# A 300-try search over instruction priorities, with new cost constants and a new load order, in a scheduled RWKV-7 and MLP kernel

## The chip, the cores and the metric

The kernel runs on one core of a Trainium2 chip. The metric is the device time of one launch in microseconds, lower is better. A core has five instruction queues that run side by side: PE (matrix multiply), DVE (vector), ACT (scalar functions), POOL (general purpose) and SP, which here does nothing but issue DMAs. Each queue executes its own instructions strictly in the order in which they stand, and waits on semaphores for the others.

## The reference

Two stages: a recurrent attention layer over 4 batches, 8 heads and 768 steps with head size 40, then an MLP with a quick GELU over the 3072 tokens that come out of it, 320 to 2048 to 320. Activations of the first stage arrive as float32, the MLP's weights as float64.

```python
for t in range(S):
    y[:, :, t] = einsum('bhd,bhde->bhe', rt, state)
    Sa = einsum('bhde,bhe->bhd', state, at)
    state = state * wt[:, :, None, :] - einsum('bhd,bhe->bhde', Sa, bt) + einsum('bhd,bhe->bhde', vt, kt)
x = y.transpose(0, 2, 1, 3).reshape(B * S, H * D)
h = x @ w_in
return (h / (1 + exp(-1.702 * h))) @ w_out
```

## The kernel before

**Tiling.** The 768 steps are cut into 12 chunks of 64, and the 4 batches into 2 pairs. A chunk of one pair is a *unit*, so there are 24 units. Unit i needs the state left by unit i-2. For each unit `decay` takes logarithms and exponentials of w, `prep` scales a, b, k and forms the score matrices (`ps_A`, `ps_RV`), `inverse` inverts a triangular matrix in five dependent levels (`ps_level`), and `solve` brings in the state (`ps_zT`, `ps_rz`, `ps_B`), solves (`ps_X`) and produces the output and the next state (`ps_y`). The output goes through a DRAM scratch (`x_dram`) and comes back transposed as `xT_all`. After both units of a chunk, `mlp` does 4 blocks of up-projection (`ps_up`, then the GELU into `g` on ACT), and two output tiles of down-projection (`ps_down`).

**Weights.** The eight pieces of float64 weights, 1.31 MB each, are loaded raw and rebuilt as float32 by one ACT instruction (L422) and five of DVE (L426, L430, L431, L434, L438). Piece n may land in a buffer that an earlier piece used (`raws`, `spots`).

**The plan.** The order of the work is not written by hand. Each piece of work is a `Task` with a priority (its *rank*, lower first), estimated durations for the engines that may do it, and dependences. `Plan.order` simulates the engines at build time: at each moment it gives each free engine the able task of lowest rank, decides the engine for tasks that may go to several, and books PSUM pairs. Its model has constants for the time in which the PE's instructions are fetched (256 at a time, `BLOCK`, `FETCH`; slower beside DMAs, `BESIDE`), for when each engine begins, and for DMA latency and rate. `Plan.paced` (L205) calls `order` four times, moving release times of the MLP tasks, and keeps the plan whose simulated end is earliest. The list it returns is emitted task by task, so that it alone fixes the order of each of the five queues. SP's queue too: a load stands in line behind all loads planned before it, and behind their waits for free buffers.

**The start.** Before the planned tasks come hand-ordered ones: the input buffers `ak`, `b`, `rv` (two of each) are set to zero once, since the loads fill only 40 of 64 rows. DVE clears the first of each and POOL the second, after it has built all masks:

```python
    for t in ak_t[1], b_t[1], rv_t[1]:
        padded(nc.gpsimd, t)
```

`load(i)` (L466 and after) plans the five loads of a unit in the order ak, time, b, rv, RV.

Of the kernel before, what the change touches and what calls it, by code (L numbers as in the profile page):

```python
# [23 lines left out]
ACT = mybir.ActivationFunctionType  # L24
# [34 lines left out]
class Plan:  # L59
# [2 lines left out]

    BLOCK, FETCH, BESIDE, AHEAD = 256, 3550.0, 0.4, 300.0
    DELAY = {"PE": 300.0, "DVE": 60.0, "ACT": 60.0, "POOL": 150.0, "SP": 800.0}

    BEGIN = {"PE": 0.0, "ACT": 3300.0, "DVE": 4100.0, "POOL": 9500.0, "SP": 800.0}
    LATENCY, RATE, SPREAD = 1200.0, 400.0, 1.3

    def __init__(self, slots, pairs):
        self.slots, self.pairs = slots, pairs
        self.tasks, self.made, self.used, self.of_pair = [], {}, {}, {}

    def add(self, rank, engines, fn, reads=(), uses=(), writes=(), room=(), pair=None, most=None, size=0):

        t = Task(rank, engines, fn, pair, most, size)
        for key in uses:  # L80
            self.used.setdefault(key, []).append(t)
        for key in reads:
            t.after.update(self.made[key])
            self.used.setdefault(key, []).append(t)
        for name, n in (*writes, *room):
            if name in self.slots:
                old = (name, n - self.slots[name])
                t.after.update(self.made.get(old, ()), self.used.get(old, ()))
        for key in writes:
            self.made.setdefault(key, []).append(t)  # L90
        if pair is not None:
            writers = self.of_pair.setdefault(pair, [])
            t.after.update(o for o in writers if "PE" in o.engines)
            writers.append(t)
        t.after.discard(t)
        self.tasks.append(t)

    def order(self):
        for n, t in enumerate(self.tasks):
            t.n, t.left, t.ready, t.then = n, len(t.after), 0.0, []  # L100
        for t in self.tasks:
            for o in t.after:
                o.then.append(t)
        free = dict(self.BEGIN)
        pairs = [0.0] * self.pairs
        held, users = {}, {k: len(v) for k, v in self.of_pair.items()}
        coming = [(t.release, t.n) for t in self.tasks if not t.left]
        heapq.heapify(coming)
        able, now, wire, out, many = [], 0.0, 0.0, [], set()
        running, last = [], {}  # L110

        def fits(t):
            if t.pair is None or t.pair in held:
                return True
            clear = sum(p <= now for p in pairs)
            if t.most is None:

                return clear > len({o.pair[0] for o in able if o.most is not None and o.pair not in held and not any(k[0] == o.pair[0] for k in many)})
            return clear > 0 and sum(k[0] == t.pair[0] for k in many) < t.most

        issued, begun, shared = 0, 0.0, 0.0

        def fetch(at):
            took = self.FETCH
            for _ in range(3):
                beside = sum(max(0.0, min(y, at + took) - max(x, at)) for x, y in running[-8:])
                took = self.FETCH + self.BESIDE / self.SPREAD * beside
            return took

        def unread(t, e):  # L130

            return max((x + 60.0 for o, x in last.get(t.pair, {}).items() if o != e), default=0.0) if t.pair is not None and e != "PE" else 0.0

        def fetched(t, start):

            at, left, ns, block = start, t.instr, t.engines["PE"] / t.instr, begun
            room = self.BLOCK - issued % self.BLOCK
            while left >= room:
                at += room * ns
                left -= room  # L140
                at = block = max(at, block + fetch(block))
                room = self.BLOCK
            return at + left * ns, block

        def ahead(t):

            return (issued % self.BLOCK + t.instr) * fetch(begun) / self.BLOCK - (now + t.engines["PE"] - begun)

        while coming or able:
            while coming and coming[0][0] <= now:  # L150
                able.append(self.tasks[heapq.heappop(coming)[1]])
            able.sort(key=lambda t: (t.rank, t.n))
            took = None
            for e in free:
                if free[e] <= now:
                    took = next((t for t in able if e in t.engines and fits(t) and unread(t, e) <= now), None)
                    if took and e == "PE" and ahead(took) > self.AHEAD:

                        took = next((t for t in able if e in t.engines and fits(t) and ahead(t) < min(self.AHEAD, ahead(took))), took)
                    if took:  # L160
                        break
            if not took:
                later = [x for x in (*free.values(), *pairs, *(unread(t, e) for t in able for e in t.engines)) if now < x < float("inf")]
                now = min(later + ([coming[0][0]] if coming else []))
                continue
            t = took
            able.remove(t)
            t.engine = e
            end = now + t.engines[e]
            if e == "PE":  # L170
                end, begun = fetched(t, now)
                issued += t.instr
            if e == "POOL" or e == "DVE" and t.sbuf:

                shared = max(now, shared) + t.engines[e]
                end = max(end, shared)
            free[e] = end
            if e == "SP":
                wire = max(wire, end + self.LATENCY)
                running.append((wire, wire + self.SPREAD * t.size / self.RATE))  # L180
                end = wire = running[-1][1]
            if t.pair is not None:
                if e != "PE":
                    last.setdefault(t.pair, {})[e] = end
                if t.pair not in held:
                    held[t.pair] = next(i for i, p in enumerate(pairs) if p <= now)
                    pairs[held[t.pair]] = float("inf")
                    if t.most is not None:
                        many.add(t.pair)
                t.bank = held[t.pair]  # L190
                users[t.pair] -= 1
                if not users[t.pair]:
                    many.discard(t.pair)
                    pairs[t.bank] = end + self.DELAY[e]
            for o in t.then:
                o.ready = max(o.ready, end + (0.0 if o.engines.keys() == {e} else self.DELAY[e]))
                o.left -= 1
                if not o.left:
                    heapq.heappush(coming, (max(o.ready, o.release), o.n))
            t.start = now  # L200
            out.append(t)
        assert len(out) == len(self.tasks)
        return out

    def paced(self, groups, rounds, window, share):  # L205
# [15 lines left out]
            vars(t).update(kept)  # L221
        return [t for t, _ in best[1]]


@with_exitstack
def rwkv7_gelu_quick(ctx: ExitStack, tc: tile.TileContext, time_d, v_d, w_d, wc_d, ak_d, b_d, rv_d, w_in, w_out, out):
    nc = tc.nc
    H, D, S = 8, 40, out.shape[0] // 4
    DM = H * D
# [11 lines left out]
    BY_PE = 4  # L241
    PLAIN = 4
    ROUNDS, WINDOW, SHARE = 4, 5000.0, 1.0
    RANKS = [14, 16, 20, 24, 35, 37, 39, 41]
    HALF = [slice(0, 64), slice(64, 128)]
    BITS = (0, 1)
# [58 lines left out]
    def padded(engine, t):  # L305
        engine.memset(t, 0.0)
# [10 lines left out]
    nc.vector.tensor_add(two32, one32, one32)  # L317
    padded(nc.vector, b_t[0])
    padded(nc.vector, rv_t[0])

    def select(t, compare, base, sign, fill):

# [13 lines left out]
    for t in logw_t:  # L336
        nc.gpsimd.memset(t[:, DM:], 0.0)

    starts = single("starts", [128, 8, 33])
    nc.gpsimd.memset(starts, 1.0)  # L340
    nc.gpsimd.memset(starts[:, :, 0], 0.0)

    quads, within = single("quads", [128, 2, 32]), single("within", [128, 2, 32])
    nc.gpsimd.memset(quads, 0.0)
# [9 lines left out]
        for p in HALF:  # L354
            select(t[p, :64], ALU.is_gt, 0, 1, 0.0)

    for t in ak_t[1], b_t[1], rv_t[1]:
        padded(nc.gpsimd, t)

    def mask(t):  # L360
        return t.unsqueeze(1).unsqueeze(1).to_broadcast([128, 2, 4, 64])
# [100 lines left out]
    def load_w(i):  # L462
        for name, of, src, n in (("wc", wc_of, wc_d, 528), ("logw", logw_of, w_d, DM))[i < BY_PE:]:
            plan.add(-2 if i == 2 else 10 * i - 30, {"SP": 350.0}, lambda t, of=of, src=src: nc.sync.dma_start(of(i), src[i]),
                     writes=[(name, i)], size=128 * n * 4)

    def load(i):
        for name, of, src, n in (("ak", ak_of, ak_d, 1024), ("time", time_of, time_d, 2 * DM), ("b", b_of, b_d, 512),
                                 ("rv", rv_of, rv_d, 1024), ("RV", RV_of, v_d, 320)):
            rows = [slice(p.start, p.start + D) for p in HALF] if name in ("ak", "b", "rv") else [slice(0, 128)]  # L470

            def go(t, name=name, of=of, src=src, rows=rows):
                for p in rows:
                    dst = of(i)[p, 8:].rearrange("p g j n -> p (g j n)") if name == "RV" else of(i)[p]
                    nc.sync.dma_start(dst, src[i, p])
            plan.add(10 * i - 4, {"SP": 350.0 * len(rows)}, go, writes=[(name, i)] + ([("v", i)] if name == "RV" else []),
                     size=sum(p.stop - p.start for p in rows) * n * 4)


    G_of = lambda i: buf("G", i, [128, 2, 160])  # L480
# [520 lines left out]
    for t in plan.tasks:  # L1001
        if t.rank >= 10000 and "PE" in t.engines:
            paces.setdefault(t.rank // 100, []).append(t)
    tasks = plan.paced(list(paces.values()), ROUNDS, WINDOW, SHARE)
    for t in tasks:
        t.fn(t)

# [80 lines left out]
```

## Time and profile before

| | us |
|---|---|
| median of 3 runs | 725.19 |
| the runs | 728.75, 724.26, 725.19 |
| the profiled execution, as timed | 728.5 |
| its span in the trace | 726.7 |

| engine | busy us | share of the span |
|---|---|---|
| PE matmul | 677.6 | 93% |
| PE weight load | 572.5 | 79% |
| DVE | 430.0 | 59% |
| ACT | 356.8 | 49% |
| POOL | 187.9 | 26% |

A row of the profile names the source line, the engine, the operation, what is written from what is read with partitions x elements, the count and the mean. Since nearly all matmuls go through one helper, they are told apart by the PSUM tile that they write. The float32 matmul of the source is two records in the trace, and each has a weight load with it. The instruction queues are themselves filled by DMA; the profile lists those packets as queue kind "instruction", and they are 16,384 bytes each.

| tile | records | columns |
|---|---|---|
| ps_up | 3840 | 256 |
| ps_down | 3072 | 320 |
| ps_level | 4000 | 32 to 128 |
| ps_y, ps_B, ps_X | 3776 | 104 |
| ps_N, ps_RV, ps_A, ps_T, ps_Q, ps_zT, ps_rz | 5248 | 32 to 64 |
| ps_cum, ps_cumc | 320 | 160, 65 |

### The profile page before, as it was taken

How to read it: one execution, taken by the hardware profiler on the slowest of the kernel's cores; microseconds unless marked ns; L12 is line 12 of the kernel's file. 1: busy time of each engine (PE TensorE's matmuls, PEld its weight loads, DVE VectorE, ACT ScalarE, POOL GpSimd, SP SyncE). 2: the span in 40 equal slices, each digit the busy share in tenths (PEclk: the TensorE clock that was granted, in tenths of full speed). 3: DMA queues.
4: the chain of work that ended last, by engine and by line, in shares of the span. 5: the costliest groups of instructions: out<-in, count | busy, mean ns of one | idle time of the engine just before them, and what ended most of it. 6: DMA issues, size and time to landing. Idle time of an engine off the chain costs nothing.

```text
span 726.7 us, 43527 instructions
## 1 busy us (share of the span) xinstructions
PE 677.6 (93%) x20256; PEld 572.5 (79%) x20256; DVE 430.0 (59%) x739; ACT 356.8 (49%) x705; POOL 187.9 (26%) x260
## 2 busy tenths in 40 slices
PE   4566997999999999999999999999999989999997
PEld 4555885799788789888888878887889978897564
DVE  6578888956667666666756655755666556431000
ACT  4455655557554554545465455457446446342120
POOL 8104143432431331330350320431530310200000
PEclk9879998999999999999999999999999999999999
DMA  7963542332251341351450440441340230110000
GB/s 216 351 251 93 165 124 86 107 96 78 91 145 55 109 120 49 88 158 32 119 136 22 116 130 31 119 118 39 120 112 23 85 95 5 40 49 30 18 5 20
DMA packets 31861, 69.82 MB, mean 96 GB/s; under 512 B 5056, under 2 KB 14272, under 8 KB 30656
## 3 DMA queue, kind: packets, MB, share of 16 engines
q1 hardware_dynamic: 31680, 67.03, 30.5%
q8 instruction: 159, 2.61, 1.4%
q14 instruction: 22, 0.18, 0.1%
HBM read 59.15 MB, written 7.86 MB: 92 GB/s over the span
## 4 chain that ended last, share of the span: by engine, by line
PE 83%; DVE 5%; issue 3%; ACT 3%; DMA 3%; POOL 2%; SPq 1%; POOLq 0%; DVEq 0%; ACTq 0%
PE ps_down L275 28%; PE ps_up L275 26%; PE ps_level L275 8%; PE ps_y L275 5%; PE ps_B L275 4%; PE ps_X L275 2%; DMA ak<-in_ak 2%; PE ps_Q L275 2%; PE ps_N L275 1%; PE ps_T L275 1%; PE ps_rz L275 1%; PE ps_A L275 1%; PE ps_RV L275 1%; PE ps_zT L275 1%; PE ps_cum L275 1%
## 5 line engine op out<-in xcount | busy, mean ns | idle before, releaser
L275 PE MATMUL ps_up<-xT_all,w_sb 64*64 64x256 f32 x3840 | 249.1, 378 | 2.6 <-ACT g L942 1.5
L275 PE MATMUL ps_down<-w_sb,g 64*64 64x320 f32 x3072 | 244.4, 434 | 3.1 <-DVE w_sb L438 2.5
L275 PEld LDWEIGHTS ps_up<-xT_all,w_sb 64*64 64x64 f32 x3840 | 160.6, 133 | 26.7 <-ACT g L942 1.8
L275 PEld LDWEIGHTS ps_down<-w_sb,g 64*64 64x64 f32 x3072 | 136.2, 134 | 45.3 <-issue 3.1
L670 ACT ACTIVATE EX<-ES,quads 128x256 f32<-128x256 f32 x116 | 52.6, 501 | 49.7 <-DVE ES L665 49.3
L591 POOL TENSOR_TENSOR kh<-time,G 128x320 f32<-128x320 f32 x24 | 22.0, 918 | 185.3 <-PE ps_y L275 91.4
L942 ACT ACTIVATE g<-ps_up 128x1024 f32<-128x1024 f32 x48 | 49.1, 1023 | 40.4 <-PE ps_up L275 40.1
L275 PEld LDWEIGHTS ps_level<-W,EX 64*64 64x64 f32 x2560 | 57.3, 134 | 7.4 <-ACT EX L670 1.4
L716 DVE TENSOR_TENSOR E<-two,ps_level 128x256 f32<-128x256 f32 x80 | 33.2, 415 | 40.3 <-ACT W L714 39.8
L275 PE MATMUL ps_level<-W,EX 64*64 64x64 f32 (+1 forms) x2560 | 55.7, 218 | 0.7 <-ACT EX L670 0.3
L714 ACT COPY W<-ps_level 128x512 f32<-128x512 f32 x51 | 29.8, 585 | 44.0 <-PE ps_level L275 43.9
L275 PE MATMUL ps_level<-PT,EX 64*64 64x64 f32 (+2 forms) x1280 | 36.6, 251 | 11.4 <-DVE EX L686 7.2
L968 DVE TENSOR_TENSOR ob<-ob,ps_down 128x320 f32<-128x320 f32 x24 | 11.6, 484 | 59.4 <-ACT ob L966 59.1
L275 PEld LDWEIGHTS ps_level<-PT,EX 64*64 64x64 f32 x1280 | 34.3, 152 | 15.2 <-DVE EX L686 7.0
L907 POOL TENSOR_TENSOR x<-zr,FT 128x128 f32<-128x128 f32 x84 | 42.8, 539 | 10.4 <-ACT zr L899 10.2
L583 POOL TENSOR_TENSOR ak<-ak,FT 128x512 f32<-128x512 f32 x21 | 27.3, 1299 | 53.2 <-DMA ak<-in_ak 26.2
L845 ACT COPY B<-ps_B 128x416 f32<-128x416 f32 x36 | 18.2, 506 | 44.1 <-PE ps_B L275 43.6
L275 PE MATMUL ps_y<-RV,kh 64*64 64x104 f32 x768 | 36.4, 252 | 2.3 <-DVE M L861 2.2
L665 DVE STREAM_TRANSPOSE ES<-E 128x256 f32<-128x256 f32 x80 | 35.6, 445 | 3.9
L275 PE MATMUL ps_y<-M,bh 64*64 64x104 f32 x768 | 36.5, 252 | 1.3 <-issue 1.3
L275 PEld LDWEIGHTS ps_y<-RV,kh 64*64 64x64 f32 x768 | 30.1, 134 | 6.4 <-DVE M L861 2.4
L861 DVE TENSOR_TENSOR M<-ps_X,later 128x832 f32<-128x832 f32 x24 | 24.5, 1021 | 17.6 <-PE ps_X L275 17.6
(140 smaller groups left out, 1132.9 us busy)
## 6 DMA issues: line engine op xcount, KB each, us to landing
ak<-in_ak SPq DMA_DIRECT2D x48, 160.0 KB
time<-in_time SPq DMA_DIRECT2D x24, 320.0 KB
rv<-in_rv SPq DMA_DIRECT2D x48, 160.0 KB
xT_all<-x_dram SPq DMA_DIRECT2D x48, 160.0 KB
wc<-in_wc SPq DMA_DIRECT2D x20, 264.0 KB
logw<-in_w SPq DMA_DIRECT2D x24, 160.0 KB
b<-in_b SPq DMA_DIRECT2D x48, 80.0 KB
RV<-in_v SPq DMA_DIRECT2D x24, 160.0 KB
```

The source lines that it names most:

```text
L275: nc.tensor.matmul(o, lhsT, rhs, start=start, stop=True, skip_group_check=True)
L583: plan.add(R, {"DVE": 690.0, "POOL": 1270.0, "sbuf": True}, lambda t: of(t.engine).tensor_mul(ahT(), ahT(), FT_of(i)), reads=T("ak", "FT") ...
L591: plan.add(R + 4, {"POOL": 870.0, "DVE": 490.0, "sbuf": True}, lambda t, n=n, dst=dst: of(t.engine).tensor_mul(dst(i)[:, :, :D], by_head(t ...
L665: plan.add(rank, dve(256), lambda t: nc.vector.transpose(ES(n), source(t)), writes=[key("ES", n, 6)], **reads)
L670: nc.scalar.activation(dst[:, :, h], ES(n), ACT.Copy, scale=quads[:, h, :1])
L714: plan.add(rank, any2(512), lambda t: copy(t.engine)(tiles_of(W(n + 1)), blocks(psum(t, ""), 64)), writes=[key("W", n + 1, 5)], pair=pair)
L716: plan.add(rank, dve(256), lambda t: nc.vector.tensor_sub(tiles_of(E(n + 1)), every(two32, [128, 2, 4, 32]), blocks(psum(t, ""), 64)[:, :, ...
L845: plan.add(R, any2(416), lambda t: copy(t.engine)(dst(), psum(t, "")[:, :, :208]), writes=[("Bv", i)] if x and c > 0 else T("B"), pair=(na ...
L861: plan.add(R + 1, dve(832), lambda t: nc.vector.tensor_tensor(M_of(i).rearrange("p (j b) n -> p b j n", b=2), psum(t, "")[:, :, :416].rear ...
L907: of(t.engine).tensor_mul(x[:, b ^ u, b], both(i)[:, at, :64], FT_of(i)[:, at])
L942: plan.add(-45, act(1024), lambda t: nc.scalar.activation(g_of(c * NQ + q).rearrange("p m r n -> p r m n"), psum(t, "").rearrange("p r (m ...
L968: plan.add(-45, dve(320), lambda t: nc.vector.tensor_add(ob_of(serial), ob_of(serial), psum(t, "")[:, 1, :DM]), reads=[("ob", serial)], wr ...
```

## The change

It does not change what is computed: the same 20,256 matmul records are issued in both programs. Five things move.

1. The constants of the model. The fetch, DMA and begin times are refitted; large loads (over 1 MB) slow the fetch more than small ones (`BESIDE_LARGE`); matmul work counts double when the PE was busy for less than 45% of the last 2.6 us (`takes`).
2. The start: DVE clears the second `b` and `rv` (`ak` stays on POOL but stands ahead of the masks), and the mask `starts` is built last.
3. The load order in a unit: ak, b, rv, RV, time; and each of the first six small loads gets a release time (`CLEAR`).
4. After `paced`, `refined` (new) tries 300 random changes of ranks, drawn from a fixed seed, and keeps each that does not make the simulated end later. A change picks 0.3 to 10% of the groups of tasks of the same kind and rank (not MLP matmuls and other extreme ranks) and adds Gaussian noise of width 0.6, 2 or 5 to their ranks; ranks of successive units are 10 apart.
5. `order` gives up and returns a short list where it can't go on; `refined` counts that as an infinite end.

```diff
-    BLOCK, FETCH, BESIDE, AHEAD = 256, 3550.0, 0.4, 300.0
+    BLOCK, FETCH, AHEAD = 256, 3528.0, 300.0
+    BESIDE, LARGE, BESIDE_LARGE = 0.35, 1e6, 0.63
+    COLD, WINDOW, SHARE = 2.0, 2600.0, 0.45
-    BEGIN = {"PE": 0.0, "ACT": 3300.0, "DVE": 4100.0, "POOL": 9500.0, "SP": 800.0}
-    LATENCY, RATE, SPREAD = 1200.0, 400.0, 1.3
+    BEGIN = {"PE": 0.0, "ACT": 3300.0, "DVE": 5500.0, "POOL": 10000.0, "SP": 800.0}
+    LATENCY, RATE, SPREAD = 2010.0, 417.0, 1.3
...
+        def takes(t, start):
+            busy = sum(max(0.0, y - max(x, start - self.WINDOW)) for x, y in worked[-60:])
+            return t.engines["PE"] * (self.COLD if busy < self.SHARE * self.WINDOW else 1.0)
...
+    def refined(self, tries, seed):
+        def end():
+            out = self.order()
+            return max(t.start + t.engines[t.engine] for t in out) if len(out) == len(self.tasks) else float("inf")
+        groups = {}
+        for t in self.tasks:
+            if abs(t.rank) < 10000:
+                groups.setdefault((t.fn.__code__.co_firstlineno, t.rank), []).append(t)
+        keys, rng, best = list(groups), random.Random(seed), end()
+        for _ in range(tries):
+            some = rng.sample(keys, max(1, int(len(keys) * rng.choice((0.003, 0.01, 0.03, 0.1)))))
+            width = rng.choice((0.6, 2.0, 5.0))
+            old = [(t, t.rank) for key in some for t in groups[key]]
+            for key in some:
+                by = rng.gauss(0.0, width)
+                for t in groups[key]:
+                    t.rank += by
+            new = end()
+            if new <= best:
+                best = new
+            else:
+                for t, rank in old:
+                    t.rank = rank
+        out = self.order()
+        return out
...
+    TRIES, SEED = 300, 4
...
     padded(nc.vector, b_t[0])
     padded(nc.vector, rv_t[0])
+    padded(nc.vector, b_t[1])
+    padded(nc.vector, rv_t[1])
...
-    starts = single("starts", [128, 8, 33])
-    nc.gpsimd.memset(starts, 1.0)
-    nc.gpsimd.memset(starts[:, :, 0], 0.0)
+    padded(nc.gpsimd, ak_t[1])
...
-    for t in ak_t[1], b_t[1], rv_t[1]:
-        padded(nc.gpsimd, t)
+    starts = single("starts", [128, 8, 33])
+    nc.gpsimd.memset(starts, 1.0)
+    nc.gpsimd.memset(starts[:, :, 0], 0.0)
...
+    CLEAR = {("ak", 0): 2000.0, ("b", 0): 3100.0, ("rv", 0): 4100.0, ("ak", 1): 4500.0, ("b", 1): 4600.0, ("rv", 1): 5500.0}
...
-        for name, of, src, n in (("ak", ak_of, ak_d, 1024), ("time", time_of, time_d, 2 * DM), ("b", b_of, b_d, 512),
-                                 ("rv", rv_of, rv_d, 1024), ("RV", RV_of, v_d, 320)):
+        for name, of, src, n in (("ak", ak_of, ak_d, 1024), ("b", b_of, b_d, 512), ("rv", rv_of, rv_d, 1024),
+                                 ("RV", RV_of, v_d, 320), ("time", time_of, time_d, 2 * DM)):
...
-                     size=sum(p.stop - p.start for p in rows) * n * 4)
+                     size=sum(p.stop - p.start for p in rows) * n * 4, release=CLEAR.get((name, i), 0.0))
...
-    tasks = plan.paced(list(paces.values()), ROUNDS, WINDOW, SHARE)
+    plan.paced(list(paces.values()), ROUNDS, WINDOW, SHARE)
+    tasks = plan.refined(TRIES, SEED)
```

What the emitted programs differ in can be counted from their instruction orders:

| | before | after |
|---|---|---|
| matmul records | 20,256 | 20,256 |
| ACT table loads | 38 | 54 |
| second-copy clears on POOL / DVE | 3 / 0 | 1 / 2 |
| first weight load, place on SP's queue | row 16 | row 16 |
| weight loads ahead of unit 2's first load | 2 | 5 |

The first twelve loads on SP before are logw, logw, ak, time, b, rv, RV, logw, ak, logw, time, b (then rv, RV); after they are logw, logw, RV, time, ak, logw, b, RV, rv, ak, b, rv (then time, logw).

More of the change, by code (lines that the diff above doesn't have):

```diff
@@ L73, in __init__, with add @@
         self.tasks, self.made, self.used, self.of_pair = [], {}, {}, {}
-    def add(self, rank, engines, fn, reads=(), uses=(), writes=(), room=(), pair=None, most=None, size=0):
+    def add(self, rank, engines, fn, reads=(), uses=(), writes=(), room=(), pair=None, most=None, size=0, release=0.0):
         t = Task(rank, engines, fn, pair, most, size)
+        t.release = release
         for key in uses:
@@ L109, in order @@
         able, now, wire, out, many = [], 0.0, 0.0, [], set()
-        running, last = [], {}
+        running, last, worked = [], {}, []
         def fits(t):
@@ L125, in fetch @@
             for _ in range(3):
-                beside = sum(max(0.0, min(y, at + took) - max(x, at)) for x, y in running[-8:])
-                took = self.FETCH + self.BESIDE / self.SPREAD * beside
+                took = self.FETCH + sum(w * max(0.0, min(y, at + took) - max(x, at)) for x, y, w in running[-10:])
             return took
@@ L132, in unread @@
             return max((x + 60.0 for o, x in last.get(t.pair, {}).items() if o != e), default=0.0) if t.pair is not None and e != "PE" else 0.0
+        def takes(t, start):
+            busy = sum(max(0.0, y - max(x, start - self.WINDOW)) for x, y in worked[-60:])
+            return t.engines["PE"] * (self.COLD if busy < self.SHARE * self.WINDOW else 1.0)
         def fetched(t, start):
-            at, left, ns, block = start, t.instr, t.engines["PE"] / t.instr, begun
+            ns = takes(t, start) / t.instr
+            at, left, block = start, t.instr, begun
             room = self.BLOCK - issued % self.BLOCK
@@ L145, in ahead @@
         def ahead(t):
-            return (issued % self.BLOCK + t.instr) * fetch(begun) / self.BLOCK - (now + t.engines["PE"] - begun)
+            return (issued % self.BLOCK + t.instr) * fetch(begun) / self.BLOCK - (now + takes(t, now) - begun)
         while coming or able:
@@ L163, in order @@
                 later = [x for x in (*free.values(), *pairs, *(unread(t, e) for t in able for e in t.engines)) if now < x < float("inf")]
-                now = min(later + ([coming[0][0]] if coming else []))
+                later += [coming[0][0]] if coming else []
+                if not later:
+                    return out
+                now = min(later)
                 continue
@@ L171, in order @@
                 end, begun = fetched(t, now)
+                worked.append((now, min(end, now + takes(t, now))))
                 issued += t.instr
@@ L179, in order @@
                 wire = max(wire, end + self.LATENCY)
-                running.append((wire, wire + self.SPREAD * t.size / self.RATE))
+                running.append((wire, wire + self.SPREAD * t.size / self.RATE, self.BESIDE_LARGE if t.size > self.LARGE else self.BESIDE))
                 end = wire = running[-1][1]
@@ L201, in order @@
             out.append(t)
-        assert len(out) == len(self.tasks)
         return out
@@ L222, in paced @@
         return [t for t, _ in best[1]]
+    def refined(self, tries, seed):
[22 more added lines that the diff above has]
+        out = self.order()
+        assert len(out) == len(self.tasks)
+        return out
 @with_exitstack
```

## The prediction

> **What bounds the kernel now.** The first table of the page says that PE is busy for 93% of the span. A busy PE is not yet a PE at its pace, so I took the pace from the densest runs in the chain of waits (start us, length us, what, records):
>
> ```profile
> 51.40 0.46 PE ps_A L275 x32
> 663.80 1.43 PE ps_y L275 x64
> 668.03 4.32 PE ps_up L275 x80
> 672.35 15.07 PE ps_down L275 x224
> ```
>
> That is 14.4 ns for a record of 64 columns or fewer, 22.3 for 104, 54.0 for 256 and 67.3 for 320. Multiplied by the records: up 3840 x 54 = 207.4, down 3072 x 67.3 = 206.7, y, B and X 3776 x 22.3 = 84.2, levels 63 (14.4 to 27 by width), the small ones 5248 x 14.4 = 75.6, sums 8: about 647 us. The change moves no record out, so 647 is the floor of both programs; 79.5 of the 726.7 are loss. Where it is follows from comparing, at the end of each unit's ps_y, the clock with the paced work done by then: unit 0 ends at 54.4 with 18.9 of work (35.5 lost), unit 1 at 65.1 with 24.5 (40.7), unit 2 at 93.3 with 44.1 (49.2), unit 3 at 134.7 with 75.0 (**59.6**), unit 23 at 665.0 with 590.4 (74.6). The last matmul starts at 721.5 (74.3); 5.2 us of stores follow. So the head loses 59.6 us in 135, the 530 us after it 15, the tail nothing but its store. The table by stages agrees:
>
> ```profile
> 0.00:12.00 12.00, 4.13 (x118) 3.81 (x122) 6.99 (x12) 5.10 (x15) 9.93 (x46) 1.00 0.66 190
> 12.00:36.00 24.00, 15.18 (x495) 13.35 (x488) 14.99 (x21) 10.08 (x27) 6.61 (x8) 0.86 0.98 330
> 36.00:60.00 24.00, 16.02 (x580) 14.17 (x584) 18.19 (x26) 14.77 (x30) 1.98 (x3) 0.79 0.62 220
> 60.00:135.00 75.00, 62.74 (x1907) 53.49 (x1902) 64.98 (x80) 41.11 (x81) 23.34 (x24) 0.91 0.36 114
> 135.00:665.00 530.00, 522.61 (x16264) 452.24 (x16260) 321.35 (x594) 277.86 (x544) 146.07 (x182) 1.00 0.29 84
> ```
>
> Columns after the length: PE, weight loads, DVE, ACT, POOL, PE clock, DMA share, GB/s. From 60 to 135 DVE is busy for 65 of 75 us: it is the bound there, and PE waits for its rebuilt weights (L438 before ps_down, at 119.3 and 130.4). From 12 to 36 the 16 DMA engines are full, and two gaps of PE have no releaser but "issue":
>
> ```profile
> 19.54 3.36 issue
> 27.12 2.82 issue
> 117.50 1.75 DVE w_sb L438
> 119.30 4.54 PE ps_down L275 x32
> ```
>
> They are waits for PE's own instructions. The queue "instruction" has 159 packets for 40,512 matmuls and weight loads, one per 255. Its packets start 3.5 us apart at the least; at 20.4, 27.5 and 34.6 us, beside the weight loads, they are 7.1 apart. Last, SP's timeline:
>
> ```profile
> 5.27 0.43 SPq L464 DMA_DIRECT2D logw<-in_w  x1
> 9.14 0.68 SPq L475 DMA_DIRECT2D ak<-in_ak  x2
> 11.64 0.66 SPq L475 DMA_DIRECT2D rv<-in_rv  x2
> 14.26 0.43 SPq L442 DMA_DIRECT2D extra<-in_w_in  x1
> ```
>
> SP stands still from 5.7 to 9.14 for POOL's clear of the second ak; unit 1's rv lands at 17.55, and the first weight load leaves at 14.26.
>
> **What the Trainium skill says.** "Perfetto Trace Analysis", Identifying the Most-Contended Engine, says that matmul busy share overstates how close PE is to its limit; agreed, 677.6 busy against 647 at pace. "TensorE: Matmul & The Clock Gate", What's actually happening: the clock is halved until PE has been busy for about 3.4 us; agreed, 0.86 and 0.79 in the two stages with long gaps, 1.00 from 135. "DMA: Bandwidth & Descriptors", Issuing engines are not separate DMA queues: all DMAs share 16 engines; agreed for instruction packets, 7.1 us apart at a DMA share of 0.98. "ScalarE: Activation LUTs", What ACT_TABLE_LOAD costs: 1283 ns and a drain of 1380; here 1283 in all 38, but FT starts at 485.49 after a load that ran from 484.19 for 1.28, so no drain shows.
>
> **The change part by part.**
>
> *Start and load order.* After, SP has no clear of POOL ahead of it but ak's, which moves ahead of the masks: logw's pads end at 3.54, plus 0.95 is 4.5. DVE's two added clears (0.49 + 0.91) end at 5.5, before zr's clears (1.67), and DVE's first useful work waits for a load until 7.0 anyway: free. SP's 18 issues through unit 1's rv, 0.40 apart from 0.81, end near 8 instead of 12.3. The data decide: before, 1.48 MB through unit 0's rv landed at 9.30, some 0.225 MB/us after 2.8 us. After, 1.97 MB stand through that rv (RV twice and a logw are ahead): 11.6, **2.3 later**; 2.79 MB through unit 1's: 15.2, **2.3 earlier**. ak and b of unit 0 come at 8.6 and 10.1 instead of 7.0 and 8.8, so unit 0's N starts about 1 us later. Before, its first level stood at 15.1 behind a DVE copy for ps_B; after, it stands behind unit 1's RV, near 16.8.
>
> *Weights and fetch.* The first weight leaves at about 9.5 instead of 14.3, and five stand together, 6.5 MB at 350 GB/s being 19 us. The slow fetches then begin one block sooner: the second block is asked for near 12.8 and comes in 5.9 to 7 us, by 19.5; the third by 26. Before, those that released PE came at 22.9, 29.9 and 37.0. From the records ahead of each block I get 3 to 4 us gained by the fourth, in spite of one more slow block (3.5).
>
> *DVE in the head.* By the mean of each row, DVE's work to the last weight is 107.1 us before, ended at 130.3: 23.2 idle, 16.8 of it before the second weight at 58.4. In the new order it is 107.5 and three kh or bh products that no row shows on DVE, 0.5 each by the nearest (L888, 491 ns): 109, **2 more**. Earlier weights and loads let me take off 5 to 8 of the idle time. Unit 3 ends at the same 75.0 of work in both orders. Taken together the head loses **5 less**; bounds -10 (15 idle left) and +8 (below).
>
> *The middle.* Cut in blocks of 128 records, 14 blocks after the 24th are shorter than a fetch of 3.53, by 3.0 us in sum; after 24 are, by 5.1: **+2**. ACT gets 16 more table loads, 20.5 us; ACT idles for half the span, and of the 38 two showed as PE waits for g (1.30 at 489.2, 0.57 at 377.3): 0.05 each, **+1**, at worst 20. Against that the paced work between dependent steps grew: levels 3.9 to 4.6 us by median, rz after zT 2.2 to 4.0, and only 4 of 19 rz instead of 8 follow within 2 us, with DVE or ACT and two semaphores between: **-3** of the some 9 us that aren't fetch. Net 0, bounds -5 and +6.
>
> *The tail.* After the last ps_y stand 300 up and 256 down matmuls of the source, 66.8 us, instead of 216 and 248, 56.7. Both run dense; the 10 us were taken from the middle, and the end moves by nothing. Cost 0; if a GELU were late there, each would show as 1 us.
>
> Sum: 726.7 - 5 + 0 = 721.7 in the trace. The profiled execution was timed at 728.5, high among the runs; the same share (723.5/728.5) of the median 725.19 gives **720**.
>
> **The rivals.** *The search reaches what it aims at.* If DVE's idle time falls to 15 (-8) and the middle's loss from 15 to 10 (-5), the time is 712. For it: every choice was drawn against the whole plan; against: DVE gets 2 us more work and short blocks grew. *The five weights in a row starve the head* (the slow side). Unit 2's rv, b and ak stand behind 6.5 MB instead of 2.6, so they land near 36; if its levels wait and one more block is fetched at 7 than I counted, units 2 and 3 lose 8 instead of winning 5; with +2 from short blocks that is +10, 735. It decides if the fourth fetch comes after 37 us. *No gain outside the plan*: the model's end is not the chip's, the gains of one stage return as waits in the next: 725.
>
> **How the numbers follow.** 1% is 7.3 us, about what can be told from no change. Forecast 0.45 (715 to 725, a third of it under 717.9), full gain 0.25, no gain 0.12, starved 0.18. Faster 0.15 + 0.25 = 0.40; within 0.30 + 0.12 = 0.42; slower 0.18. A tenth on each side leaves 710 to 734.
>
> **What would show it.** SP without a hole before 9 us; unit 1's rv near 15; the issue gaps of PE earlier by 3 and no more than two; the last L438 by 126; lost time at unit 3 near 55; 54 table loads with few PE waits on g; from 135 on a loss of 12 to 18. A loss at unit 3 over 60, or over 20 after it, makes me wrong.

## The result, and the profile after

The changed kernel takes **734.11 us** (732.62 to 734.41) beside 725.57 of the kernel before on the same chips: a ratio of 1.0115, 95% interval 1.0086 to 1.0145. It is slower by 8.5 us; the forecast was 720, faster than before. The profiled execution was timed at 734.41, its span is 732.7 and its PE busy time 677.6, as before: all of the difference is PE waiting. By stages (columns as in the prediction's table):

```profile
12.00:36.00 24.00, 15.60 (x522) 13.62 (x514) 16.20 (x23) 12.05 (x29) 3.92 (x5) 0.93 0.98 370
36.00:60.00 24.00, 15.55 (x552) 14.24 (x552) 21.92 (x23) 12.97 (x27) 8.08 (x5) 0.79 0.48 153
60.00:135.00 75.00, 64.33 (x2054) 52.91 (x2057) 64.27 (x96) 42.67 (x79) 26.73 (x25) 0.98 0.41 127
135.00:665.00 530.00, 516.25 (x16046) 437.32 (x16041) 316.85 (x584) 287.50 (x538) 153.25 (x193) 1.00 0.29 83
```

Compare the last line with that of the kernel before: in the same 530 us PE is busy for 516.3 instead of 522.6, and ACT for 287.5 instead of 277.9. So the time was lost in the middle. Its loss can be split. I went through PE's records after 135 us, laid each at the pace of its width behind the one before, and put each late start to what released it (a late start is the time by which a record begins after the one before it should have ended at its pace). Both kernels were profiled twice (the second time as b_before and a_after below):

| loss, us | before, two profiles | after, two profiles |
|---|---|---|
| head, to the end of unit 3 | 59.6, 58.9 | 55.3, 59.5 |
| late after 135 us, in sum | 15.0, 17.6 | 25.2, 23.3 |
| of it released by ACT | 2.2, 2.1 | 8.3, 8.1 |
| of it without a releaser (instruction fetch) | 4.9, 7.9 | 9.5, 7.7 |
| of it all others | 7.9, 7.6 | 7.4, 7.5 |
| span | 726.7, 728.6 | 732.7, 734.8 |

By the means: head -1.9, middle +8.0, and of that ACT +6.1, fetch +2.2, others -0.3. The spans differ by 6.1 in the mean and the medians by 8.5, since both profiles of the kernel before are of executions above its median. The waits on ACT differ by 6 between the kernels and by 0.2 at most between two profiles of one; for the head and for the fetch, two profiles of one kernel lie further apart (55.3 and 59.5; 4.9 and 7.9) than the means of the two kernels.

That gaps without a releaser are waits for instructions can be read from the packets of the queue "instruction": of the 10 such gaps longer than 0.15 us after 135 us in the kernel before, all end 1.2 to 1.6 us after a packet has come in, though packets come only every 4.1 us there; in the changed kernel 16 of 21 do, with 8.0 of their 8.9 us.

Among the waits of PE between 135 and 665 us, these are the rows on ACT, first before, then after (what waited, for what, us in total, times, longest):

```profile
PE ps_up L275 <- ACT g L942: 1.5, 2, 1.1
```

```profile
PE ps_RV L318 <- ACT g L988: 2.5, 2, 1.9
PE ps_up L318 <- ACT G L602: 1.3, 1, 1.3
PE ps_level L318 <- ACT W L760: 0.9, 1, 0.9
PE ps_rz L318 <- ACT zT L858: 0.7, 1, 0.7
PE ps_RV L318 <- ACT W L760: 0.6, 1, 0.6
```

What ACT did before the longest of them is in the chain of waits of the changed kernel (start us, length us, what):

```profile
324.76 1.02 ACT g L988
...
325.79 1.28 ACT L602
...
327.54 1.28 ACT L538
...
328.84 0.65 ACT wc L538
...
329.84 0.48 ACT W L760
...
330.80 0.44 DVE ES L711
...
331.63 1.03 ACT g L988
332.66 0.04 issue
332.70 0.69 PE ps_RV L318 x32
```

L602 and L538 without a tile are table loads (ACT_TABLE_LOAD in the trace, here where the activation differs in kind from the one before). L602 is the exponential G, L538 the logarithm. A GELU was planned between a unit's exponentials and its G. So G needs a load, the logarithm needs another, and the next GELU a third; W, which a level needs, and that next GELU, whose PSUM PE wants, stand behind. All 54 loads take 1283 ns, as the 38 before did.

Of the 16 new loads, 5 stand at a G (6 instead of 1), 6 at a logarithm (7 instead of 1) and 5 at a GELU (20 instead of 15). The six G loads begin at 166.7, 222.4, 267.1, 325.8, 384.5 and 520.2 us, and 7.0 us of PE's late starts on ACT lie within 9 us of one of them: most of the loss on ACT stands at the six places where a GELU splits a unit's exponentials.

### The profile page after: what moved, and what is told of

The parts are those of the page before. It is cut to its first block, busy times and chain, and to the rows that moved or that the text cites. A ratio compares the mean times of both kernels' runs of the same rounds, so it can differ in the third digit from the quotient of the medians.

```text
span 732.7 us, 43540 instructions
## 1 busy us (share of the span) xinstructions
PE 677.6 (92%) x20256; PEld 567.4 (77%) x20256; DVE 429.6 (59%) x739; ACT 369.3 (50%) x697; POOL 201.9 (28%) x272
## 4 chain that ended last, share of the span: by engine, by line
PE 76%; ACT 10%; DVE 5%; DMA 4%; issue 3%; POOL 1%; SPq 1%; DVEq 0%; ACTq 0%
PE ps_down L318 26%; PE ps_up L318 22%; PE ps_level L318 7%; PE ps_y L318 4%; PE ps_B L318 4%; PE ps_X L318 2%; ACT g L988 2%; PE ps_T L318 2%; ACT L988 2%; PE ps_N L318 1%; PE ps_RV L318 1%; PE ps_Q L318 1%; PE ps_rz L318 1%; DMA extra<-in_w_out 1%; PE ps_A L318 1%
## 5 line engine op out<-in xcount | busy, mean ns | idle before, releaser
L318 PEld LDWEIGHTS ps_up<-xT_all,w_sb 64*64 64x64 f32 x3840 | 157.6, 133 | 29.9 <-issue 1.5
L318 PEld LDWEIGHTS ps_down<-w_sb,g 64*64 64x64 f32 x3072 | 139.1, 133 | 41.2 <-issue 3.6
L988 ACT ACTIVATE g<-ps_up 128x1024 f32<-128x1024 f32 x48 | 49.2, 1026 | 58.5 <-PE ps_up L318 58.2
L716 ACT ACTIVATE EX<-ES,quads 128x256 f32<-128x256 f32 x100 | 45.6, 504 | 41.5 <-DVE ES L711 39.7
L637 POOL TENSOR_TENSOR kh<-time,G 128x320 f32<-128x320 f32 x22 | 20.1, 911 | 168.1 <-issue 98.6
L760 ACT COPY W<-ps_level 128x512 f32<-128x512 f32 x55 | 32.2, 585 | 42.8 <-PE ps_level L318 41.9
L953 POOL TENSOR_TENSOR x<-zr,FT 128x128 f32<-128x128 f32 x84 | 44.9, 564 | 29.2 <-ACT EX L716 17.7
L1014 DVE TENSOR_TENSOR ob<-ob,ps_down 128x320 f32<-128x320 f32 x24 | 11.6, 481 | 68.5 <-ACT ob L1012 68.3
L891 ACT COPY B<-ps_B 128x416 f32<-128x416 f32 x39 | 19.8, 507 | 62.6 <-PE ps_B L318 62.4
L718 POOL TENSOR_TENSOR EX<-ES,quads 128x512 f32<-128x512 f32 x19 | 26.8, 1411 | 39.9 <-DVE ES L711 29.8
```

Of the source, the lines that this page charges most:

```text
L318: nc.tensor.matmul(o, lhsT, rhs, start=start, stop=True, skip_group_check=True)
L637: plan.add(R + 4, {"POOL": 870.0, "DVE": 490.0, "sbuf": True}, lambda t, n=n, dst=dst: of(t.engine).tensor_mul(dst(i)[:, :, :D], by_head(t ...
L716: nc.scalar.activation(dst[:, :, h], ES(n), ACT.Copy, scale=quads[:, h, :1])
L718: of(t.engine).tensor_mul(dst, ES(n).unsqueeze(2).to_broadcast([128, 8, 2, 32]), quads.unsqueeze(1).to_broadcast([128, 8, 2, 32]))
L760: plan.add(rank, any2(512), lambda t: copy(t.engine)(tiles_of(W(n + 1)), blocks(psum(t, ""), 64)), writes=[key("W", n + 1, 5)], pair=pair)
L891: plan.add(R, any2(416), lambda t: copy(t.engine)(dst(), psum(t, "")[:, :, :208]), writes=[("Bv", i)] if x and c > 0 else T("B"), pair=(na ...
```

## The experiments

Two theories at first. **Theory 1**: table switches on ACT hold up PE. **Theory 2**: instruction fetch in short blocks does. Times are medians beside the kernel before (723.9 to 725.6 in these runs); the last two columns are from one profile each.

| run | time | ratio to before, 95% | late after 135: ACT, no releaser | lost at unit 3 |
|---|---|---|---|---|
| e_hoist | 735.94 | 1.0136 (1.0091-1.0181) | 6.3, 12.3 | 57.3 |
| e_loads | 738.36 | 1.0163 (1.0117-1.0210) | 13.0, 8.2 | 56.9 |
| n_before | 723.12 | 0.9971 (0.9946-0.9997) | 0.7, 6.4 | 54.6 |
| n_after | 727.23 | 1.0009 (0.9983-1.0035) | 0.2, 10.8 | 57.8 |
| e_start | 746.06 | 1.0296 (1.0255-1.0337) | 9.3, 8.1 | 63.9 |
| h_clear | 724.27 | 0.9971 (0.9951-0.9991) | 2.1, 4.1 | 54.9 |
| e_notries | 731.08 | 1.0071 (1.0045-1.0097) | 3.3, 8.9 | 54.9 |
| e_searchold | 728.97 | 1.0040 (1.0002-1.0077) | 6.9, 7.5 | 55.5 |
| f_notries | 727.73 | 1.0039 (1.0017-1.0062) | 0.7, 8.1 | 58.8 |
| f_table | 714.48 | 0.9869 (0.9808-0.9930) | 0.1, 6.7 | 49.2 |
| f_again | 715.29 | 0.9886 (0.9852-0.9920) | 0.6, 3.2 | 50.2 |
| a_after | 734.63 | 1.0130 (1.0077-1.0184) | 8.1, 7.7 | 59.5 |

**Fewer loads in the same order of PE** (e_hoist).

```diff
+        early[i - 2, 1] = plan.tasks[-1]
...
+        early[i, 0] = plan.tasks[-1]
...
     tasks = plan.refined(TRIES, SEED)
+    for key in sorted(early):
+        t = early[key]
+        if key[0] >= EARLY:
+            old = tasks.index(t)
+            new = 1 + max(tasks.index(o) for o in t.after)
+            if new < old:
+                tasks.insert(new, tasks.pop(old))
```

> The changed kernel with one edit: in units 4 to 23 the exponential G and the two logarithms that follow it are emitted as soon as what they read has been emitted, so they stand directly behind the other exponentials of their unit and no GELU comes between. Table loads fall from 54 to 35; PE's order is the same record by record. Theory 1 (table loads on ACT are what the middle lost): the loss from 135 us on falls from 25 to 16-19, the median from 734 to 725-728. Theory 2 (instruction fetch in short blocks): nothing of it is touched, the loss stays at 23-26 and the median at 732-735.

A miss for theory 1: 735.9 with 19 loads fewer, and 6.3 us of waits on ACT are left of 8.2. ACT's timeline in this kernel shows why:

```profile
263.99 0.63 ACT L594 ACTIVATE FT<-wc 128x512 f32<-128x512 f32 x1
264.53 0.61 ACT L595 ACTIVATE GT<-wc 128x512 f32<-128x512 f32 x1
...
266.11 0.46 ACT L541 ACTIVATE logw<-logw 128x320 f32<-128x320 f32 x1
266.59 1.28 ACT L992 ACT_TABLE_LOAD   x1
267.88 1.02 ACT L992 ACTIVATE g<-ps_up 128x1024 f32<-128x1024 f32 x1
```

The GELU that had gone first now stands behind the whole run of exponentials and logarithms, and ps_B waited 1.5 us for it, until 269.0. So the number of loads is not the price; theory 1 has to be put otherwise: what counts is what ACT has ahead of the work that PE waits for. The time is in the range of theory 2, and the fetch gaps of this profile are 12.3 us; whether they are more than chance one profile cannot tell.

**Loads ahead of GELUs** (e_loads).

```diff
+                if c * NQ + q in (9, 14, 18, 23, 27, 32, 36, 41):
+                    nc.scalar.preload_act_table_set("natural_log_exp_and_others")
                 nc.scalar.activation(
```

> The kernel before with 8 extra table switches, each right ahead of one of the 48 GELUs in the middle (13 more loads in all, 51 instead of 38). Nothing else moves. Theory 1: each load costs PE about 0.4 us as in the changed kernel (6 us for 16), so the median rises by 4-6 us to 729-732. Theory 2, and the price used in the prediction (0.05 us each): it rises by under 1 us.

It rose by 13.3 us, more than either theory gave: 1.0 us for each of the 13 loads. PE was late on all eight of these GELUs, by 11.3 us in sum at the pace; the largest among the waits of PE on them:

```profile
PE ps_level L275 <- ACT g L945: 2.9, 2, 1.7
PE ps_cum L275 <- ACT g L945: 2.0, 1, 2.0
PE ps_N L275 <- ACT g L945: 1.5, 2, 1.2
PE ps_up L275 <- ACT g L945: 1.1, 2, 0.7
```

ACT is idle for half the span, and yet a load at this place is paid for with 1.0 of its 1.28 us.

**No table switches in either kernel** (n_before, n_after). Both leave the GELU out of the computation.

```diff
-            if i >= EARLY:
-                nc.scalar.preload_act_table_set("natural_log_exp_and_others")
...
-                ACT.Gelu_apprx_sigmoid), writes=[("g", c * NQ + q)], pair=("up", c * NQ + q))
+                ACT.Copy), writes=[("g", c * NQ + q)], pair=("up", c * NQ + q))
```

> The kernel before without any table switch: the GELU is replaced by a plain copy (the activation is left out of the computation) and the explicit table loads go, so one load of 38 stays. Order unchanged. Theory 1 (table switches delay PE through ACT): 5 to 10 us less than the kernel before, 715-720. Theory 2 (instruction fetch): within 2 us of it.

> The changed kernel with the same two edits (GELU left out, one table load of 54 stays), order unchanged. Theory 1: the difference to the kernel before without switches shrinks from 8.5 us to between -4 and +3, as the head's gain stays: 714-721. Theory 2: it keeps its distance of 7-10 us to the other one.

Orders unchanged, one load left in each, and the copy takes as long on ACT as the GELU (median 1023 ns beside 1025), so only the loads are gone. The distance between the two falls from 8.5 to 4.1 us by medians, and from 1.15% to 0.38% (1.0009 beside 0.9971), 2.8 us, by ratios. n_before fell by 2.2 us, short of theory 1's 5 to 10 and beside theory 2's 2, but it had only 2.2 us of waits on ACT to lose. Neither expectation of n_after was met whole. The waits on ACT are gone (8.2 to 0.2; no row of them among PE's waits in the middle), so the switches carry some 4 to 6 us of the difference. What makes the rest is not shown: the fetch gaps, 10.8 beside 6.4, are as large as it, but those of one kernel differed by 3.0 between two executions. The head's gain isn't there (57.8 beside 54.6).

**The start** (e_start, h_clear). e_start has the new clears and load order on the old plan; h_clear the clears alone (with the mask `starts` built last):

```diff
     padded(nc.vector, rv_t[0])
+    padded(nc.vector, b_t[1])
+    padded(nc.vector, rv_t[1])
...
+    padded(nc.gpsimd, ak_t[1])
...
-    for t in ak_t[1], b_t[1], rv_t[1]:
-        padded(nc.gpsimd, t)
```

> The kernel before with the new clears at the start and the new order of loads in a unit alone; old constants, no search. If the head's gain of 4 comes from them: lost 54-57 at unit 3, median 720-724. If it comes from the fitted constants or the search: lost 58-61 at unit 3, median 724-728. It has 50 table loads; by theory 1 its middle then loses 3-5 more than before, by theory 2 nothing more.

> The kernel before with the new clears alone (b and rv of the second buffers on DVE, ak's ahead of POOL's masks); load order, constants and plan as before, so every queue has the order of before but for the clears. By the step of the prediction: the hole of SP from 5.7 to 9.1 us closes, unit 1's rv lands 3 us earlier, the slow fetches start earlier; lost at unit 3 falls from 59 to 55-57, median 721-724. Rival (DVE is the bound of the head, so that PE's earlier start comes to nothing): 724-727.

e_start met neither expectation: 746, with 63.9 lost at unit 3. A new load order makes the plan rearrange every queue (50 table loads, 9.3 us of waits on ACT), so this run doesn't isolate the start. h_clear does, since the clears are outside the plan. SP's timeline in it, beside that shown before:

```profile
5.27 0.43 SPq L465 DMA_DIRECT2D logw<-in_w  x1
6.19 1.31 SPq L476 DMA_DIRECT2D ak<-in_ak  x2
...
10.15 1.07 SPq L476 DMA_DIRECT2D rv<-in_rv  x2
...
12.90 0.42 SPq L443 DMA_DIRECT2D extra<-in_w_in  x1
```

The hole is closed, unit 1 ends at 61.8 instead of 65.1 and 64.5, and 54.9 are lost at unit 3 instead of 59.6 and 58.9. e_loads, which is the kernel before up to its first added load at 214.5 us, lost 56.9 there; so by single profiles the gain of the head is 2 to 5 us. The two medians differ by 0.8 us, the ratio by 0.29%, 2.1 us: 724.27 lies in the rival's range, just outside the other.

**Search or constants** (e_notries: the changed kernel with `TRIES = 0`; e_searchold: the kernel before with `refined` alone).

> The changed kernel with 0 instead of 300 tries: new constants, start and load order, but the plan as the pacing leaves it. 42 table loads, 18 short blocks of 3.7 us in sum. If the search made the loss of the middle: head about as in the changed kernel (lost 54-58 at unit 3), middle 14-18, median 720-726. If the new constants made it: middle 22-26, median 731-735.

> The kernel before with the search of 300 tries alone, on the old constants, clears and load order. 49 table loads. If the search on a plan that does not know the tables gives back what it wins, as in the changed kernel: 724-736, PE's waits on ACT after 135 us at 4 to 9. If the new constants are at fault: 715-722.

The constants, clears and load order without the search are already slower than before by 0.7%, within the range given for "the new constants made it", with 3.3 us of waits on ACT and 8.9 of fetch gaps. So the larger part of the change's 1.15% does not need the search, and which of constants and load order makes it stays open (e_start, the load order on the old constants, was slower by 3.0%). The search on the old plan is slower by 0.4%, with 6.9 us of waits on ACT, as expected of a plan that does not know the tables. With seed 4 the search adds such waits with either constants: 2.2 become 6.9, 3.3 become 8.3.

**A plan that knows the tables** (f_table, again as f_again; f_notries without tries).

```diff
-        issued, begun, shared = 0, 0.0, 0.0
+        issued, begun, shared, table = 0, 0.0, 0.0, "N"
...
             end = now + t.engines[e]
+            if e == "ACT" and t.table:
+                ok, to = t.table
+                if table not in ok:
+                    end, table = end + 1290.0, to
```

GELU gets `table=("S", "S")`, G `("NE", "E")`, the logarithms `("NL", "L")`, a unit's exponentials `("", "N")`; the flat 1300 on the last two go.

> The changed kernel with one thing added to the plan's model: it keeps the state of ACT's tables and charges 1.29 us where a GELU, G or logarithm needs another one, instead of flat 1.3 us on the exponentials and logarithms. The search of 300 tries is the same. 44 table loads, 17 short blocks of 4.3 us. Theory 1: ACT's waits are seen by the plan, PE's waits on ACT after 135 us fall from 8 to about 3, median 723-729. Theory 2: 730-735.

> The changed kernel with the table state in the model and 0 tries. 39 table loads. Beside the same without the table state (731, PE's waits on ACT 3.3): if the state alone helps, 722-728 with waits under 2; if it needs the search, 728-733. Beside the three seeds with it (714, 721, 730) it tells what the draws add.

> The kernel with the table state in the plan's model and seed 4 once more, unchanged, since its first timing rests on four runs. If it is the fastest of these versions: 712-719, PE's waits on ACT after 135 us under 1 again. If the first runs were favourable by chance: 720 or more.

f_table beats both kernels, twice, and lies below both ranges given. After 135 us only DVE and fetch are left among the waits of PE (the three largest shown):

```profile
PE ps_X L322 <- issue: 0.8, 1, 0.8
PE ps_level L322 <- issue: 0.7, 2, 0.5
PE ps_up L322 <- DVE W L764: 0.4, 1, 0.4
```

It still has 44 loads, six more than the kernel before; they have a place. But its head is 9 us better too, and the waits on ACT can't explain that. The table state without tries (f_notries) came where it was expected, 727.73 with 0.7 us of waits on ACT: hardly better than 731.08 without the state (the intervals, 1.0017-1.0062 and 1.0045-1.0097, overlap). So the gain of f_table needs the search, and the draws were tried.

**Other seeds** (`SEED` 5 and 6, each without and with the table state).

> The changed kernel with seed 5 in place of 4: another draw of the 300 tries. 43 table loads, 19 short blocks. If the plan that doesn't know the tables can't tell good draws from bad ones: 724-736. If seed 4 was merely unlucky and the search works: 712-722.

> The changed kernel with seed 6: 55 table loads (one more than with seed 4), 15 short blocks. If table switches at the wrong place are the price: 730-738, the worst of the two new seeds. If they are not: no worse than seed 5.

> The kernel with the table state in the plan's model, seed 5. If knowing the tables is what made seed 4 fast: 711-720. If seed 4 was a lucky draw: 722-733, as the changed kernel's seeds.

> The kernel with the table state in the plan's model, seed 6. If knowing the tables is what made seed 4 fast: 711-720, PE's waits on ACT after 135 us under 3. If seed 4 was a lucky draw: 722-733.

| seed | plan without the tables | ACT waits | plan with them | ACT waits |
|---|---|---|---|---|
| 4 | 1.0115 (1.0086-1.0145) | 8.3 | 0.9869 (0.9808-0.9930) | 0.1 |
| 5 | 1.0060 (1.0036-1.0084) | 2.4 | 0.9951 (0.9929-0.9973) | 1.3 |
| 6 | 1.0068 (1.0047-1.0089) | 5.1 | 1.0066 (1.0038-1.0094) | 0.1 |

With the table state the waits on ACT are lower with every seed. It doesn't decide the time alone: f_seed5's 721.10 lies between the two ranges given, f_seed6's 729.79 in that of a lucky seed 4. The means are 1.0081 and 0.9962; with three seeds each, and 2% between the best and the worst draw, how much of f_table's 0.9869 is its seed stays open (medians without the tables: 734.11, 728.48, 730.45; with them: 714.48, 721.10, 729.79). What seed 6 waits for instead can be seen in its one profile, though that is of the longest of its 20 executions (737.7): gaps without a releaser longer than 0.15 us add up to 14.6 us after 135 us, 13.6 of them 1.2 to 1.6 us after an instruction packet, where the changed kernel had 8.9. Whether its median execution has as many is not known.

Without the tables, the search gained nothing on the chip that can be told from chance: the ratios are 1.0071 without tries, 1.0115, 1.0060 and 1.0068 with them. a_seed6 has most loads of all (55) and 730.45 is at the edge of its expected 730 to 738, yet it is not worse than seed 5 by more than the intervals. For the second profiles:

> The kernel before once more, unchanged, for a second profile on the chip of these runs: it tells how far the losses of one kernel differ between two executions. Expected: lost at unit 3 within 3 us of 59.6, after it within 3 of 15, gaps without a releaser within 3 of 4.9.

> The changed kernel once more, unchanged, for a second profile. Expected: PE's waits on ACT after 135 us within 1 of 8.3, gaps without a releaser within 3 of 9.5, lost at unit 3 within 3 of 55.3; median within 3 of 734.

They put the spread of one kernel's fetch gaps at 2 to 3 us and of its head at up to 4 (a_after's head, 59.5, missed its expectation); a head read from one profile can't show a smaller difference.

## Why the prediction was wrong

**The step that failed** is the table loads in the middle: "0.05 each, +1, at worst 20". Measured were +6.1 us of waits on ACT for 16 loads, 0.4 each, and 1.0 each where they stand right ahead of a GELU. With it the middle, forecast at 0, lost 8.0 more by the means of two profiles. I had averaged the two waits seen over all 38 loads of the kernel before. But in that kernel most loads were at places with slack, and the new ones were not like them: the plan charges a flat 1.3 us to the exponentials and logarithms of each unit and nothing to a GELU or a G, so an order with a GELU in between has up to three loads more than the plan charges. With 300 tries on the model's end, gains that the model only imagines can be kept. The search is not alone in it, though: without any try the change is slower by 0.7%, with 42 loads and 3.3 us of waits on ACT, and where the rest of that comes from stays open. ACT's idle half was no cover, since ACT works in order and the loads came in runs (three of 1.28 us between 325.8 and 331.6). The upper bound was in the text, the range of the middle (-5 to +6) did not use it.

**The second wrong term** is the "-3" for longer distances between dependent steps: the waits on DVE, POOL and small ones went from 7.8 to 7.5 only. That distances had grown where little waited is a guess; no run tests it.

**Short blocks**, "+2": fetch gaps went from 6.4 to 8.6 in the means, right in size, though two profiles of one kernel differ by as much.

**The head**, "5 less": 55.3 in the first profile looks right, 59.5 in the second doesn't; the mean gain is 1.9, within the spread of one kernel. The two rv loads came as worked out (unit 0's released its matmul at 10.6 and 10.9, forecast 11.6; unit 1's at 15.5, forecast 15.2). The first weight did not: it left at 12.6 and 12.9, not near 9.5. The gaps without a releaser ended at 18.3, 25.1 and 31.2 instead of 22.9, 29.9 and 37.0, earlier than I had said, and in the second profile at 19.7 and 32.2. Yet unit 1 ended at 66.3 and 70.9, later than before. PE's X of unit 1 was 3.9 us late for T, and DVE's timeline shows what T stood behind:

```profile
52.88 1.54 DVE L470 TENSOR_SCALAR w_sb<-w_sb 128x1280 f32<-128x1280 f32 x1
54.46 1.38 DVE L474 TENSOR_SCALAR w_sb<-w_sb 128x1280 int32<-128x1280 int32 x1
55.87 1.38 DVE L475 TENSOR_SCALAR w_sb<-w_sb 128x1280 int32<-128x1280 int32 x1
57.17 1.48 DVE L478 SCALAR_TENSOR_TENSOR w_sb<-w_sb 128x1280 f32<-128x1280 uint32 x1
58.68 1.49 DVE L482 TENSOR_TENSOR w_sb<-w_sb 128x1280 f32<-128x1280 f32 x1
...
60.90 0.48 DVE L833 SCALAR_TENSOR_TENSOR T<-ps_T,quads,T 128x256 f32<-128x256 f32 x1
```

PE had ended ps_T, which T reads, at 57.7. A whole weight was put ahead of T, and its first three steps took 1.4 to 1.5 us each instead of the 0.8 that the same steps took for the weight at 39.3 us. I had summed DVE's work to the last weight and not what stood ahead of unit 1. In h_clear, where DVE's order is that of before, unit 1 ends 3 us earlier, which fits; no run moves this weight alone.

**The tail**, 0: right; the last matmul starts 5.2 us before the end in both.

**The floor.** The terms that I listed for the paced work add up to 645 us, not 647. Both kernels have the same records, so no difference between them depends on it.

**The rivals.** The one on the slow side named 735, near the time, by another mechanism: five weights in a row starving the fetch. That did not happen, the fetch came earlier; that its number is near is luck. The rival of no gain, 725, named gains that return as waits, but no loss on top. The rival of full gain named 712: f_table's 714 to 715 is reached when the plan knows the tables, with one seed of three. Of the signs for the head, SP without a long hole and unit 1's rv near 15 came; the last weight was done at 126.0 in the first profile but at 130.1 in the second (before 130.3), and the gaps of PE for instructions were three in the first, not at most two. The sign that would "make me wrong", over 20 lost after unit 3, is what came: 25.2 and 23.3.

## What to carry to other kernels

A search over a plan exploits what the plan leaves out, so the question to ask of it is not how much it can gain but which costs it can create for nothing; here they were counted beforehand (16 table loads) and priced wrongly. Without the tables in its model the search gained nothing that could be measured here with any of three seeds. A cost that the old kernel pays where there is slack gives no price for the same cost at a new place: look at what stands behind it in its queue and who waits for that. And fix the model before drawing, and draw more than once: the state of the tables took a few lines of the plan, and with it the waits on ACT fell to at most 1.3 us with all three seeds; yet the times of these seeds still lay 2% apart.

## What the runs showed of the hardware

An activation that goes back to the exponential after a GELU loads a table set that does not serve the logarithm that follows: G's load at 325.79 is followed by the logarithm's own at 327.54, 1.28 us each. This came at all six G loads of the changed kernel. In e_hoist, where G and the logarithms follow the other exponentials, no load stands between them (263.99 to 266.57).

PE's instructions come in by DMA and can hold it up: in the kernel before their packets started 3.3 us apart at the least (not 3.5, as I had read), and 7.1 apart at 27.5 and 34.6 us, beside the weight loads. The waits vary from one execution to the next: gaps of PE without a releaser differed by 3.0 us between two executions of the same program (4.9 and 7.9).
